# Half-size products for one more up-projection and one more down-projection, attention in pairs of PSUM banks, merged stores and a new order

## The chip, the core and the metric

The kernel runs on one core of one Trainium2 chip. The time is device microseconds of one execution of the whole program. The engines are called PE (TensorE, matmuls; PEld are its weight loads), DVE (VectorE), ACT (ScalarE), POOL (GpSimd, which here only issues the loads and builds one iota) and SP (SyncE, which issues stores and DMA transposes). PSUM has eight banks of 512 fp32 numbers in each of 128 partitions; a matmul writes into one bank.

## What is computed

```python
# q, k, v: [8 batches, 8 heads, 576 positions, 64] fp32; w_in: [512, 2048]; w_out: [2048, 512]
scores = q @ k.T / 8  - slope[h] * |i - j|       # only where 0 <= i - j < 128
attn   = softmax(scores) @ v                     # window of 128
x = attn, heads side by side                     # [4608 tokens, 512]
out = relu(x @ w_in) ** 2 @ w_out                # [4608, 512] fp32
```

## The kernel before

**Tiling.** The tokens are cut into blocks of 128 positions of one batch (the fifth block of a batch has 64; two of these share one tile). Nine groups of four tiles (512 tokens) go through the two projections. Attention of a block multiplies its queries with the keys of its own and of the preceding block: `scores` (L631) fills four PSUM banks `a`, two heads of 256 columns in each; four exponentials (`expo`, L668) and four mask multiplications (`mask`, L675) make `P`; two `pv` steps (L740), each in one bank, multiply with the values and, by a column of ones, give the sums of each row; a reciprocal (L766) and a normalisation (L771) for each of the two write `x`. The first eight blocks, one of each batch, have no predecessor: four of them are done alone (`lone`, L691, with their bias added by a matmul), four in pairs. Their operands are transposed on PE (`tp`, `xp`), those of all later blocks by DMA transposes on SP (L568, L784). A block `m` is numbered in the order in which it is done.

**Up-projection.** `UNITS` and `unit` (L882) do groups 0 to 2 in pieces of 128 or 256 tokens, `fc_step` (L907) groups 3 to 5 in 16 steps of four matmuls of 512 columns. Groups 6 to 8 (`G_UP = 6`) go through `up_product` (L968): a 2 x 2 block product done with seven products of half-size blocks in place of eight (the Strassen-Winograd scheme). Each of four passes `u` has seven products `p`, in the order 1, 2, 6, 5, 7, 3, 4, of four matmuls of 256 columns. The running sums in two PSUM banks X and Y are copied out (`snap`: s1, s2, s5, to `cs` buffers that lie in `vf`, the values of the first blocks) and added to (c11, c22, c12). The block sums of the weights are made once (`up_weight_sums`, L927), those of the tokens for each group (`prepare_up`, L948). `relu_square` (L851) then makes `g` = relu squared: a relu on ACT, a square on DVE or, from group 4 on, on either.

**Down-projection.** Group 0 (`G_STR = 1`) goes through `o_part` (L1054): four tiles x four parts of four matmuls of 512 columns, each part needing only its own quarter of `g` and of `w_out`. Groups 1 to 8 go through `product` (L1126), again seven products, each in two halves of eight matmuls of 256 columns. Products 5, 6, 7 and 4 take sums of quarters of `g`, eight additions on DVE made by `prepare` (L1267): S1, S2, S3, S4; the sums of `w_out` (`wsum`) are made once by `weight_sums` (L1103). Four results are copied to `osb` buffers, three additions finish them, and each tile's half row is stored by one DMA on SP, two where a tile holds two blocks of 64. The last group's product 4 is cut in three (`last_product`, L1230) so that only 128 columns are left at the end.

**What sets the order.** Every step is a task with an engine (or a choice of two), a duration, dependencies, buffers that it takes and gives back (`Slot`) and a key. `Plan.order` (L166) walks through a modelled time and gives each engine, of the tasks that could start next, the one with the smallest key; the resulting order is what each engine's program is. `DUE` gives the first blocks' attention keys near -1e5, loads are near -9e6 and -1e6, projection steps count up from 0. `ADJ` (L54) adds a number written by hand to the keys of some 350 tasks, so `"xp7.0": 129923.5` puts the output transpose of block 7 behind everything that could run. `FIRST` (L17) orders the first loads, all issued by POOL. The `xT` buffer holds three groups: `x` of a tile is written when the up-projection three groups earlier has ended.

PSUM is given out as two banks `h`, one `ox`, one `oy` and four `a` (L342).

Of the kernel before, what the change touches and what calls it, by code (L numbers as in the profile page):

```python
# [38 lines left out]
G_STR = 1  # L39
G_A = 8  # L40
XR = 12
OSB = 5
LAST = 128
G_UP = 6
# [4 lines left out]
RT = 4  # L49
# [5 lines left out]
    "S1.3.0": -903.7, "S1.7.0": 70758.5, "S2.1.0": -1115, "S2.2.1": -558.9, "S2.5.0": 156718, "S3.1.1":  # L55
    105994.9, "S4.1.1": -173131.7, "S4.2.0": 630.1, "S4.5.1": 159840.4, "S4.7.0": 66819.9, "S4.7.1": 198631.5,
    "c22.6.0": -5759.8, "c22.6.2": -2129.9, "c22.7.2": -1777, "c22_4": -255.5, "c22_7": 15343.5, "c22_8":
    -78636.1, "e0.1": 111206.1, "e1.0": 23715.8, "e1.1": -8901146.1, "e11.3": -64325.5, "e12.1": 1217.7,
    "e13.3": 1606.1, "e17.3": 101005.7, "e21.3": 24.9, "e22.1": -48173, "e22.2": -25260.8, "e24.3": 169638.3,
    "e25.1": 163276.8, "e27.1": -198977.9, "e27.2": -1687.7, "e28.0": -234769.8, "e29.1": -301187, "e33.1":  # L60
    124529.3, "e33.2": 227823.7, "e35.3": 124434.7, "e36.1": 10272.4, "e36.2": 2557.9, "e36.3": 7965.3, "e38.2":
    -149, "e38.3": -1670.7, "e6.1": -1247.6, "e9.2": 65398.4, "e9.3": 1738.8, "ev0.1.2": 111234.6, "f6.0.1":
    -988.6, "f6.0.2": -98587.6, "f6.0.3": 116086, "f6.0.5": -98595.7, "f6.0.6": -999.6, "f6.0.7": -13071.6,
    "f6.1.1": -65.1, "f6.1.2": -37683.3, "f6.1.3": -33.7, "f6.1.7": -24308.9, "f6.2.3": 1139.9, "f6.3.2":
    1356.9, "f6.3.3": -316324.9, "f6.3.4": -321979.8, "f7.0.5": 54.9, "f7.1.2": -14751.5, "f7.1.3": 25461.6,
    "f7.1.6": 202.7, "f7.2.3": 25643.8, "f7.2.5": -430.7, "f7.3.2": 244.8, "f7.3.3": 562.7, "f8.0.1": 25806.8,
    "f8.0.3": 520.3, "f8.0.4": 4161.1, "f8.1.3": 30.7, "f8.2.6": -111.1, "f8.2.7": 303.1, "f8.3.3": -159.7,
    "f8.3.4": -94.8, "fc3.1": -41390.5, "fc3.11": -108694.5, "fc3.12": 8034.2, "fc3.13": -177, "fc3.14": 2926.1,
    "fc3.3": -1137.3, "fc3.4": 2862, "fc3.6": -36.5, "fc3.7": -13287.6, "fc3.8": -1157.7, "fc3.9": 11910.5,
    "fc4.0": 12316.7, "fc4.1": 74.1, "fc4.10": 1558, "fc4.11": -1365.7, "fc4.12": 237.6, "fc4.15": -53227.4,  # L70
    "fc4.2": 579.5, "fc4.3": -4010, "fc4.4": -4017, "fc4.6": 267.5, "fc4.7": -1190.4, "fc4.8": -1343.7, "fc4.9":
    -1123, "fc5.1": -184989.8, "fc5.12": -185595.5, "fc5.13": 34045.7, "fc5.14": 896.9, "fc5.15": 734.1,
    "fc5.6": -186223.5, "fc5.7": 661.3, "fc5.9": -186903.9, "kqT16": -174448, "kqT17": 1852.3, "kqT33": -3670.1,
    "kqT34": -2892.3, "lk0.1": 93144.3, "lkq10": -7921038.5, "lkq11": -7921244.2, "lkq12": -7921029.2, "lkq13":
    -7921040.5, "lkq15": -7921000.4, "lkq22": -4.8, "lkq33": 4.3, "lkq36": 181.3, "lkq37": 41384.2, "lkq38":
    -1.7, "lkq8": -7923174.6, "lkq9": -7923136.2, "lv0": -396.5, "lv1": 171.2, "lv10": -7921242.9, "lv20": 3.5,
    "lv28": 993.2, "lv31": 5317.9, "lv36": 41385.5, "lv37": 44238.4, "lv38": 116727.7, "lv39": 41330.6, "lv4":
    1104, "lv6": 75443.5, "lv7": 75344, "lv9": -8025976.9, "m10.0": -1285.4, "m10.1": -30579.1, "m17.0": 2349.5,
    "m17.3": 78002.3, "m21.3": -747.7, "m24.1": 6701.1, "m27.1": 4083.6, "m34.2": 3159.8, "m34.3": 1215.9,
    "m35.0": 1081, "m36.1": 40372.7, "m38.0": 184007.6, "m38.2": 258320.9, "mask0.4": 98879.3, "mask0.5":  # L80
    98879.3, "mask1.3": -1706.3, "mask1.5": -1028.7, "n30.1": 774.5, "n34.0": 10378, "n35.0": 157747.2,
    "o0.0.1": 208.3, "o0.1.2": -72.7, "o0.2.1": 555.9, "o0.3.2": 1297.6, "oe0.0.0": -100128.9, "p1.1.1":
    281063.6, "p1.4.0": 127651.2, "p1.4.1": 879.6, "p2.1.0": -1203, "p2.1.1": 1469.8, "p2.3.0": -41470.3,
    "p2.4.1": 11452.2, "p2.7.1": -1427.4, "p3.1.1": 11949.8, "p3.5.0": 275.6, "p3.6.0": -295, "p3.6.1": -1332.8,
    "p3.7.0": -872.6, "p4.2.0": -1102, "p4.2.1": 92382.6, "p4.3.0": 34421.9, "p4.5.0": 98082.2, "p4.5.1": 476.9,
    "p4.6.0": -213, "p4.6.1": -152.3, "p4.7.1": -508, "p5.2.1": -361.7, "p5.4.0": 62539.3, "p5.5.0": -24602.7,
    "p5.5.1": 463.1, "p6.3.0": 22388.1, "p6.3.1": -722.6, "p6.6.0": 78.7, "p6.6.1": 23875.2, "p6.7.1": 25992,
    "p7.2.0": 4145.8, "p7.3.0": 10821.9, "p7.4.0": 41877.9, "p7.5.1": 43365.4, "p7.6.0": 4154, "p7.6.1":
    43379.9, "p7.7.1": 310.4, "p8.1.0": -76542.9, "p8.5.1": -18573.3, "pv0.1": -23357.1, "pv12.1": -522.7,
    "pv14.0": 625.5, "pv16.1": 1283, "pv19.0": -32.7, "pv19.1": -44115, "pv20.0": 5439.4, "pv20.1": 5438.4,  # L90
    "pv21.0": 9095.4, "pv24.0": -201.1, "pv24.1": -4445, "pv25.1": 1375.7, "pv27.0": 99651, "pv29.1": 92442.5,
    "pv33.0": 481.4, "pv33.1": 3237.8, "pv37.1": 177519.5, "pv4.0": 99332, "pv6.1": 98100.8, "pv7.0": 98916.4,
    "pv7.1": 99166.1, "pv8.0": 164078.1, "r15.0": 1175.1, "r17.1": -6146.6, "r25.1": 3291.9, "r29.0": 4221.8,
    "r30.1": 301.5, "r33.0": -12604, "r35.0": 107764.7, "reluc11.8.2": -274, "reluc12.7.2": -50123.6,
    "reluc12.8.0": 32.4, "reluc22.7.1": -11320.1, "reluf6.3.4": -3847.6, "reluf7.0.4": -10523.3, "reluf7.2.4":
    69.1, "reluf8.1.4": -79957.9, "relufc3.2": -980.7, "relufc3.3": -6110.2, "relufc3.6": -195912.8,
    "relufc4.1": -184059.9, "relufc4.13": -235858.7, "relufc4.2": -5773.1, "relufc5.12": -88019.4, "reluu0.0.3":
    -100507, "reluu0.1.0": -120967.3, "reluu0.1.2": -3207.6, "reluu0.2.0": -99526.1, "reluu2.0.0": 4286.3,
    "reluu2.1.4": -8799.1, "s1.6.1": -1465.9, "s1.7.1": -11303, "s1.7.3": -2349.5, "s18": -769.6, "s1_3":
    -269.1, "s2.6.1": -1027.6, "s2.8.0": -1755, "s20": -7708.7, "s37": 117244.8, "s38": 1255.1, "s5.6.2": -1466,  # L100
    "s5.7.1": -11322.8, "s5.8.0": -209.7, "s5_4": -17186.6, "s5_5": -1045.8, "s8": 1235.4, "sqc11.6.0": 12346,
    "sqc11.6.2": 117202.1, "sqc11.8.2": -61412.6, "sqc11.8.3": 57564.4, "sqc12.6.3": 181517.6, "sqc22.6.0":
    83950, "sqc22.8.1": -88695.8, "sqc22.8.2": 5878.9, "sqf6.1.4": 485.3, "sqf7.0.4": -11305.2, "sqfc4.0":
    55950.5, "sqfc5.12": -1038.8, "squ2.1.6": -663.5, "tp4.0": 99371.5, "tp6.0": 99111.2, "u0.0.4": -888.6,
    "u0.1.3": -790.9, "u0.2.3": -42892.5, "u0.3.3": -937.1, "u1.0.1": -43010.8, "u1.0.3": 31757.8, "u1.0.4":
    -11117.2, "u1.0.6": -10920.4, "u1.1.3": -986.2, "u1.1.4": -910.9, "u1.1.6": -858.6, "u1.1.7": -111184.8,
    "u2.0.0": 219.9, "u2.0.1": 8321.7, "u2.0.2": -57842.5, "u2.0.5": -58325.1, "u2.0.7": -1666.5, "u2.1.0":
    -1151.3, "u2.1.2": -1538.6, "u2.1.3": 110.2, "u2.1.4": -1181.8, "u2.1.5": -1561.6, "u2.1.6": -571.8,
    "u2.1.7": -577.8, "us1.1": 17891.1, "us1.2": 157040.1, "us3.0": -23.7, "us3.1": -21539.9, "us3.3": 2091,
    "ut6.0": -937.1, "ut6.2": -742.1, "w_in0": 532.9, "w_in1": -166.6, "w_in2": -313.3, "w_in3": -413.7,  # L110
    "w_out2": -272.8, "w_out3": 119.4, "x16": 3186.3, "xp5.0": 56027.3, "xp6.0": 99154.6, "xp7.0": 129923.5,
# [18 lines left out]

class Slot:


    def __init__(self, tag):
        self.tag, self.tile, self.left, self.freed, self.idx, self.turn = tag, None, 0, 0.0, 0, 0


class Plan:


    LAT = {"PE": 210.0, "ACT": 180.0, "DVE": 190.0, "POOL": 200.0, "SP": 200.0, "ACTQ": 200.0}
    SELF = {"ACT": 120.0, "DVE": 110.0}
# [123 lines left out]
def kernel(  # L266
# [23 lines left out]
    for b in range(0, B, 2):  # L290
        for x in [(b + i, kb) for i in range(2) for kb in range(1, HALF)]:
            jobs.append(("full", [len(seq)]))
            seq.append(x)
            ranges.append([x])
        jobs.append(("half", [len(seq), len(seq) + 1]))
        seq += [(b, HALF), (b + 1, HALF)]

        ranges.insert(len(ranges) - (b + 2 == B), seq[-2:])
# [58 lines left out]
    def tile_of(slot):  # L357
        return tiles[slot.tag][slot.idx]

    def act(n):  # L360
        return n * 0.832 + 51.0
# [980 lines left out]
```

## Time and profile before

| | us |
|---|---|
| median of three runs (300.56, 301.49, 301.82) | 301.49 |
| the profiled execution's own time | 302.54 |
| its span in the profile | 300.8 |
| PE busy, of the span | 288.8 |
| DVE busy | 243.3 |
| ACT busy | 205.2 |
| POOL busy (issuing loads) | 106.5 |

The profile is that of the one execution in the second row. Busy times are sums over the whole span; the page also cuts the span into 40 slices of 7.5 us and gives each engine's busy share of a slice in tenths. PEclk is the granted clock of TensorE in the same slices. Groups of instructions are listed by line, engine and tiles as count, busy time, mean length of one in ns, idle time before them and who ended it. In the timeline a line has start, length, engine, line, operation, tiles and count, and in brackets the idle time before it. The PE stages by time: group 0 goes up from 15.9 to 34.5 us, group 1 from 49.6 to 71.2, groups 3, 4 and 5 from 118.4, 139.8 and 170.0, groups 6, 7 and 8 from 205.8, 234.5 and 259.6; the last product ends at 295.3.

### The profile page before, as it was taken

How to read it: one execution, taken by the hardware profiler on the slowest of the kernel's cores; microseconds unless marked ns; L12 is line 12 of the kernel's file. 1: busy time of each engine (PE TensorE's matmuls, PEld its weight loads, DVE VectorE, ACT ScalarE, POOL GpSimd, SP SyncE). 2: the span in 40 equal slices, each digit the busy share in tenths (PEclk: the TensorE clock that was granted, in tenths of full speed). 3: DMA queues.
4: the chain of work that ended last, by engine and by line, in shares of the span. 5: the costliest groups of instructions: out<-in, count | busy, mean ns of one | idle time of the engine just before them, and what ended most of it. 6: DMA issues, size and time to landing. Idle time of an engine off the chain costs nothing.

```text
span 300.8 us, 8326 instructions
## 1 busy us (share of the span) xinstructions
PE 288.8 (96%) x3279; PEld 226.2 (75%) x3299; DVE 243.3 (81%) x628; ACT 205.2 (68%) x390; POOL 106.5 (35%) x132
## 2 busy tenths in 40 slices
PE   8799999997999999999999999999999999999992
PEld 4588757886888888556576776568888888888882
DVE  5567568679877899688799997699989998999852
ACT  2685445576487673785978747896979669888710
POOL 8944488445551585522639205510000000000000
PEclk9999999999799999999999999999999999999999
DMA  9999999999999999999999999996103101110213
GB/s 126 170 201 206 181 190 159 164 173 174 174 167 186 123 130 187 164 157 140 167 187 179 160 191 166 152 158 107 37 17 109 38 35 37 70 37 0 80 61 108
DMA packets 170920, 39.62 MB, mean 132 GB/s; under 512 B 156928, under 2 KB 170368, under 8 KB 170880
## 3 DMA queue, kind: packets, MB, share of 16 engines
q0 software_dynamic: 115184, 18.10, 86.5%
q1 hardware_dynamic: 55264, 20.66, 39.2%
q8 instruction: 26, 0.43, 0.6%
q10 hardware_dynamic: 432, 0.33, 0.4%
q14 instruction: 14, 0.11, 0.1%
HBM read 36.70 MB, written 9.44 MB: 153 GB/s over the span
## 4 chain that ended last, share of the span: by engine, by line
PE 85%; DMA 5%; POOL 5%; DVE 2%; issue 1%; POOLq 0%
PE o L1158 33%; PE h L914 14%; PE h L995 12%; PE h L896 10%; PE pv L749 6%; PE s L642 5%; DMA w_in_sb<-in_moe_w_in_dram 5%; PE o L1071 4%; POOL kq L522 2%; POOL vf L527 1%; POOL w_in_sb L467 1%; DVE sums L1281 1%; PE tp L583 1%; PE o L1241 1%; DVE g L869 1%
## 5 line engine op out<-in xcount | busy, mean ns | idle before, releaser
L857 ACT ACTIVATE rt<-h 128x512 bf16<-128x512 f32 (+1 forms) x109 | 64.4, 595 | 30.6 <-PE h L896 14.8
L669 ACT ACTIVATE P<-s 128x512 bf16<-128x512 f32 x120 | 63.6, 604 | 12.7 <-PE s L642 12.7
L1158 PEld LDWEIGHTS <-g 128*128 128x128 bf16 x624 | 59.5, 98 | 8.2
L869 DVE TENSOR_TENSOR g<-rt 128x512 bf16<-128x512 bf16 (+1 forms) x101 | 41.7, 415 | 20.1 <-ACT rt L857 18.6
L522 POOL DMA_DIRECT2D kq<-in_k_dram x39 | 33.2, 852 | 54.0 <-DMA kqT<-kq 47.4
L1158 PE MATMUL o<-w_out_sb,g 128*128 128x256 bf16 x384 | 47.2, 273 | 0.0
L896 PE MATMUL h<-xT,w_in_sb 128*128 128x128 bf16 (+1 forms) x512 | 46.6, 246 | 0.4 <-DMA w_in_sb<-in_moe_w_in_dram 0.4
L914 PE MATMUL h<-xT,w_in_sb 128*128 128x512 bf16 x178 | 45.0, 379 | 0.7
L896 PEld LDWEIGHTS <-w_in_sb 128*128 128x128 bf16 x512 | 38.6, 98 | 4.2 <-DMA w_in_sb<-in_moe_w_in_dram 0.6
L677 DVE TENSOR_TENSOR P<-P,masks 128x512 bf16<-128x512 bf16 x96 | 38.3, 416 | 3.1 <-ACT P L669 1.2
L527 POOL DMA_DIRECT2D vt<-in_v_dram x32 | 27.1, 855 | 31.5 <-PE pv L749 30.7
L522 POOL DMA_DIRECT2D kq<-in_q_dram x39 | 33.6, 862 | 7.7 <-PE h L896 3.2
L1158 PE MATMUL o<-wsum,sums 128*128 128x256 bf16 x256 | 32.9, 279 | 2.1 <-DVE sums L1281 2.1
L777 DVE TENSOR_TENSOR x<-pv,rec 128x256 bf16<-128x256 f32 (+1 forms) x80 | 31.7, 413 | 0.7
L1158 PE MATMUL o<-wsum,g 128*128 128x256 bf16 x240 | 30.7, 273 | 0.0
L1158 PEld LDWEIGHTS <-sums 128*128 128x128 bf16 x256 | 25.1, 100 | 6.6 <-DVE sums L1281 2.3
L914 PEld LDWEIGHTS <-w_in_sb 128*128 128x128 bf16 x192 | 17.2, 98 | 16.6
L749 PEld LDWEIGHTS <-P 128*128 128x128 bf16 (+1 forms) x576 | 23.7, 101 | 6.2 <-issue 0.9
L867 ACT ACTIVATE g<-rt 128x512 bf16<-128x512 bf16 x44 | 27.6, 629 | 1.1
L857 ACT ACTIVATE rt<-vf 128x512 bf16<-128x512 f32 x36 | 22.5, 626 | 6.2 <-DVE vf L1016 5.8
L1016 DVE TENSOR_TENSOR vf<-h,vf 128x512 f32<-128x512 f32 x36 | 24.2, 685 | 2.6 <-PE h L995 2.2
L376 ACT ACTIVATE osb<-o 128x512 f32<-128x512 f32 x21 | 12.6, 598 | 17.1 <-PE o L1158 14.8
(81 smaller groups left out, 393.5 us busy)
## 6 DMA issues: line engine op xcount, KB each, us to landing
out_dram<-osb SPq DMA_DIRECT2D x55, 128.0 KB, 2.7
kq<-in_k_dram POOLq DMA_DIRECT2D x31, 128.0 KB, 7.0
kq<-in_q_dram POOLq DMA_DIRECT2D x31, 128.0 KB, 7.5
vt<-in_v_dram POOLq DMA_DIRECT2D x24, 128.0 KB, 7.5
w_out_sb<-in_moe_w_out_dram POOLq DMA_DIRECT2D x4, 512.0 KB, 14.6
w_in_sb<-in_moe_w_in_dram POOLq DMA_DIRECT2D x3, 512.0 KB, 10.6
out_dram<-osb SPq DMA_DIRECT2D x17, 64.0 KB, 2.1
vf<-in_v_dram POOLq DMA_DIRECT2D x8, 128.0 KB, 6.9
```

Source lines behind the costliest of these rows:

```text
L522: nc.gpsimd.dma_start(view(kq[s_kq[m].idx], i), source(src, m, split))
L527: nc.gpsimd.dma_start(tile_of(s_v[m])[0:n, :, 0:D], source(v, m))
L669: nc.scalar.activation(flat(Pt[sP.idx]), sS[i].tile.rearrange("p (j t) -> p j t", j=2)[:, :, lo:hi], AF.Exp, bias=0.0, scale=scale)
L677: nc.vector.tensor_tensor(flat(Pt[sP.idx]), flat(Pt[sP.idx]), flat(masks), op=ALU.mult)
L749: nc.tensor.matmul(sv.tile[0:n, hi * (D + 1):(hi + 1) * (D + 1)], prob, tile_of(s_v[mk])[:, h, 0:D + 1], start=mk == parts[0][1], stop=mk ...
L777: nc.vector.tensor_tensor(o, heads(sv)[0:n, :, 0:D], sr.tile[0:n, :].unsqueeze(2).to_broadcast([n, 4, D]), op=ALU.mult)
L857: nc.scalar.activation(srt.tile[:, 0:n], i, AF.Relu, bias=0.0, scale=1.0)
L869: nc.vector.tensor_tensor(o, i, i, op=ALU.mult)
L896: nc.tensor.matmul(slot.tile[:, f * w:(f + 1) * w], w_in_sb[:, cc, fc * 128:(fc + 1) * 128], xT[:, cc, lo % (XR * 128):lo % (XR * 128) + w ...
L914: nc.tensor.matmul(slot.tile, w_in_sb[:, cc, fc * 128:(fc + 1) * 128], xT[:, cc, g * 512 % (XR * 128):g * 512 % (XR * 128) + 512], start=c ...
L995: nc.tensor.matmul(slot.tile[:, j * 256:j * 256 + 256], a, b_, start=fresh and j == 0 and c == 0, stop=c == 1, skip_group_check=True)
L1158: nc.tensor.matmul(slot.tile[:, z * 256:z * 256 + 256], stationary(c), moving(c), start=fresh and z == 0 and c == 0, stop=c == F - 1, skip ...
```

## The change

- Group 5 goes up in half-size products too (`G_UP = 5`), and group 0 comes down in them (`G_STR = 0`). The copies' buffers `cs` are four in `vf` and two of their own; one output buffer and one relu buffer fewer (`OSB`, `RT`).
- The four `a` banks become two pairs. One exponential and one mask multiplication cover four heads (1024 columns) in place of two; the two `pv` steps of a block share a pair and have one reciprocal and one normalisation. In the last groups X and Y of a product share a pair. Some products and scores get a dependency that keeps PE's order.
- Stores of two neighbouring tiles are one DMA, and so are the two halves of a tile of 64-row blocks. In the last group the stores of product 3 and of the first 128 columns of the last tile go to ACT's queue, the very last to SP's. The tile with two 64-row blocks of the last batches moves from place 34 to place 32 of 36, so the last two tiles are neighbours.
- All entries of `ADJ` are replaced by others; among the early tasks, those of pv4, pv6, pv7, xp5, xp6 and xp7 are gone, and the iota, the first loads and the squares of group 0 have new ones.

The core of the diff, with entries of `ADJ` that matter early:

```diff
-G_STR = 1
+G_STR = 0
-OSB = 5
+OSB = 4
-G_UP = 6
+G_UP = 5
-RT = 4
+RT = 3
+CS_V = 4
+CS = 6
...
-    "pv4.0": 99332, "pv6.1": 98100.8, "pv7.0": 98916.4, "pv7.1": 99166.1,
-    "tp4.0": 99371.5, "tp6.0": 99111.2, "xp5.0": 56027.3, "xp6.0": 99154.6, "xp7.0": 129923.5,
+    "iota": -12415.8, "lkq1": -13499.7, "lv0": -13699.2, "lv1": -13798.7, "w_in1": -14029.7,
+    "lkq6": 149813.3, "lv4": 149948.7, "lv5": 149915.9, "lv6": 7870399.3, "lv7": 149679.6, "xp4.0": -47745.1,
...
-    psum_bufs = {"h": 2, "ox": 1, "oy": 1, "a": 4}
+    psum_bufs = {"h": 2, "ox": 1, "oy": 1, "a": 2}
...
-        slot.tile = psum.tile([128, 512], FP32, tag=slot.tag, bufs=psum_bufs[slot.tag], name=name)
+        slot.tile = psum.tile([128, 2, 512] if slot.tag == "a" else [128, 512], FP32, tag=slot.tag,
+                              bufs=psum_bufs[slot.tag], name=name)
...
-        sS = [Slot("a") for _ in range(4)]
+        sS = [Slot("a") for _ in range(2)]
...
-            deps = [last["s"]]
+            deps = [last["s"], t_last.get(j - 2)]
...
-        cols = 2 * (hi - lo)
-        for i in range(4):
-            w = slice(2 * i, 2 * i + 2)
+        cols = 4 * (hi - lo)
+        for i in range(2):
+            w = slice(4 * i, 4 * i + 4)
...
+            def norm():
+                nc.vector.tensor_tensor(
+                    xt[sx.idx][0:n, :].rearrange("p (b h e) -> p b h e", b=2, h=4), both()[:, :, :, 0:D],
+                    sr.tile[0:n].unsqueeze(3).to_broadcast([n, 2, 4, D]), op=ALU.mult)
...
+            st["Y"], st["done"] = st["X"] if tag == "a" else Slot(tag), {"before": last.get("s5")}
...
+    def places(r, n):
+
+        rows = [[b * S + kb * 128 for b, kb in ranges[r + i]] for i in range(n)]
+        if n == 2 and len(rows[0]) == len(rows[1]) == 1:
+            lo, d = rows[0][0], rows[1][0] - rows[0][0]
+            if d >= 128 and lo + 2 * d <= NT:
+                return [((0, 1), lambda w: out[lo:lo + 2 * d, w].rearrange("(j p) c -> p j c", p=d)[0:128])]
...
+        if p == 1 and g - 1 in strassen:
+            need = need + [strassen[g - 1]["P", 5, 0]]
+        if p == 5:
+            need = need + [st["P", 2, 0]]
...
+            for i, (j, to) in enumerate(places(4 * g + tok, 2)):
+                def run(j=j, to=to):
+                    (nc.scalar if end else nc.sync).dma_start(
...
+            q = z == 1 and lo == 0
+
+            def store(lo=lo, hi=hi, q=q):
+                to = places(4 * g + 2 + z, 1)[0][1]
+                (nc.scalar if q else nc.sync).dma_start(to(slice(lo, hi)), so.tile[:, z * 256 + lo:z * 256 + hi])
```

## The prediction

> **What bounds the kernel now.** I read the page's busy times and slices first, then the chain of waits, then the stretches and the timeline where the slices dip.
>
> ```profile
> PE 288.8 (96%) x3279; PEld 226.2 (75%) x3299; DVE 243.3 (81%) x628; ACT 205.2 (68%) x390; POOL 106.5 (35%) x132
> ...
> PE   8799999997999999999999999999999999999992
> ...
> DVE  5567568679877899688799997699989998999852
> ...
> PEclk9999999999799999999999999999999999999999
> ```
>
> PE is full in all slices but the first two, the eleventh (about 75 us) and the last. A full slice can still be slow, so I took the pitch of matmuls from long unbroken pieces of the chain (start, length, line, count):
>
> ```profile
> 39.75 1.73 PE o L1071 x8
> ...
> 283.03 10.48 PE o L1158 x96
> ```
>
> A matmul of 512 columns costs 1.73/8 = 0.216 us, one of 256 costs 10.48/96 = 0.109 us. At these pitches the full slices hold little but work: **PE's own work is the bound from 16 to 295 us**. A cut of PE work shows in the end time only if the other engines feed PE as fast as before. Three places are not PE work: the start (to 16 us, untouched in kind), one stall, and the tail after the last matmul.
>
> ```profile
> 71.71 0.69 DVE L1281 TENSOR_TENSOR sums<-g 128x1024 bf16<-128x1024 bf16 x1
> 72.31 0.42 DVE L869 TENSOR_TENSOR g<-rt 128x512 bf16<-128x512 bf16 x1
> 72.65 0.68 DVE L1281 TENSOR_TENSOR sums<-sums,g 128x1024 bf16<-128x1024 bf16 x1
> 73.25 0.69 DVE L1281 TENSOR_TENSOR sums<-g 128x1024 bf16<-128x1024 bf16 x1
> ...
> 73.99 2.52 PE L1158 MATMUL o<-wsum,sums 128*128 128x256 bf16 x16 [2.08 <-DVE sums L1281]
> ```
>
> The first group that is multiplied in half-size products (group 1) makes PE wait 2.08 us for the sums of its operands; behind it the 16 matmuls take 2.52 us where 16 x 0.109 = 1.75 are due, because the granted clock halves (0.79 over 72 to 80 us). Together the stall costs about 3.9 us.
>
> **Products (PE).** Group 0's down-projection: 64 matmuls of 512 columns (64 x 0.216 = 13.86 us) become 7 products of 16 matmuls of 256 columns (112 x 0.109 = 12.23): **-1.63**. Group 5's up-projection is the same exchange: **-1.63**. The weight loads grow by 48 a group at 0.098 us each, but lie beside the matmuls: in the all-product stretch (206 to 283 us) they are busy 68.3 of 77 us and PE is full.
>
> Here a rule speaks against the change. The Trainium skill ("TensorE: Matmul & The Clock Gate", section "Back-to-back issue gap") gives a sustained spacing with weight loads of about 81 ns at 128 columns and 131 ns at 512. An estimate between them, 98 ns at 256, would make each exchange 64 x 0.131 = 8.4 against 112 x 0.098 = 11.0 us, +2.6 a group. The trace contradicts it: 216 and 109 ns, weight loads included.
>
> **Attention in pairs (ACT, DVE).** Rows used (count, busy, mean ns):
>
> ```profile
> L669 ACT ACTIVATE P<-s 128x512 bf16<-128x512 f32 x120 | 63.6, 604 | 12.7 <-PE s L642 12.7
> L677 DVE TENSOR_TENSOR P<-P,masks 128x512 bf16<-128x512 bf16 x96 | 38.3, 416 | 3.1 <-ACT P L669 1.2
> L1281 DVE TENSOR_TENSOR sums<-g 128x1024 bf16<-128x1024 bf16 x16 | 11.0, 687 | 0.4 <-ACT g L867 0.2
> L1016 DVE TENSOR_TENSOR vf<-h,vf 128x512 f32<-128x512 f32 x36 | 24.2, 685 | 2.6 <-PE h L995 2.2
> ```
>
> Four exponentials of 512 become two of 1024. No row has one; the 256- and 512-column relus take 0.384 and 0.599, so 1024 is estimated at 1.03 (between 0.60 and 1.21, two of today's). Over 30 jobs: 30 x (4 x 0.604 - 2 x 1.03) = 10.7 us less ACT. Masks: 120 x 0.416 to 60 x 0.687, -8.7. Reciprocals 72 to 36 at 0.17, -6.1. Normalisations 72 x 0.413 to 36 x 0.685 (the PSUM row), -5.1. DVE -19.9 in all. PE's attention work stays.
>
> **What the products add.** Group 5: 12 additions at 0.685 = 8.2, four token sums at 0.41 = 1.6 (DVE), 12 copies at about 0.64 = 7.7 on either engine. Group 0: eight sums at 0.685 = 5.5, three additions = 2.05; four copies replace four. So DVE stands at about +1, ACT at -7: over the kernel a wash. The place matters.
>
> ```profile
> 170.00:206.00 36.00, 35.74 (x425) 24.73 (x429) 31.39 (x92) 26.12 (x48) 9.31 (x12) 1.00 1.52 166
> 206.00:283.00 77.00, 77.00 (x796) 68.32 (x794) 72.44 (x144) 63.55 (x113) 0.00 (x0) 1.00 0.16 47
> ```
>
> (Columns: length, then busy PE, PEld, DVE, ACT.) Group 5's up-projection runs in the first stretch. DVE and ACT there hold 31.4 + 26.1 = 57.5 us. Add 8.2 + 1.6 + 7.7, take off 1.1 (weight sums that must now come earlier) and 6.7 (nine blocks of attention: 3.8 DVE, 2.9 ACT): 67.2 of 2 x 34.4 = 68.8, or 98%. From 206 to 283 us PE was full with these engines at 136/154 = 88%. Between 88% and 98% lies the risk: nothing, if work slides on; 5.8 us, if all the copies' half share and today's squares stay on DVE (31.4 + 8.2 + 1.6 + 4.1 - 1.1 - 3.8 = 40.2 against 34.4). Nearest is the full-PE row, and squares may go to ACT (L870): I take **+1.0**.
>
> **Early stage.** Group 0's old down-projection was free filler: its 16 parts need no sums. Its new products 5, 6, 7 and 4 need sums on DVE, products 2, 3 and 7 the last of w_out, which landed at 37.5 us. The last up-matmul of group 0 ends at 34.5, its square at 35.6; the two S1 sums with one between (as at 71.71 to 73.94) add 2.2: product 5 starts at 37.9. PE has only product 1 (1.75) and a transpose (0.45) till then, so 1.2 us idle, or 2.9 if product 1 ran earlier, as its counterpart did: I take +2.9. Against it: today block 7's output transpose runs at 61.47, though its operand was ready at 58.5; 24 product matmuls went first, by an order entry of +129923.5 on xp7.0. The entry is gone, as are those on pv4, pv6, pv7 and xp6. Group 1's second half (62.6 to 71.2) can then start about 3 us earlier, and its sums too, while group 0's later products fill: -3.9 for the stall. Sum **-1.0**; from -3.9 (no new stall) to +6.2 (below). Moving the iota behind five load issues (0.87 each) makes the first scores later by some 0.5 and the first loads earlier by 0.5: nothing.
>
> The clock weighs here. The trace halved it for some 3.4 us (0.79 over 8 us) behind a wait of 2.08. The same page of the Trainium skill ("Why this matters for your kernels") warns of gaps over about 3 us only; by that rule neither stall would cost clock, by the row each costs 1.7 more. The -3.9 holds the row's price.
>
> **Tail.** One queue issues the last stores in series:
>
> ```profile
> 293.15 3.21 SPq L1196 DMA_DIRECT2D out_dram<-osb  x5
> 296.47 1.74 SPq L1258 DMA_DIRECT2D out_dram<-osb  x3
> ...
> 295.31 0.29 DVE L1251 TENSOR_TENSOR osb<-osb,o 128x128 f32<-128x128 f32 x1 [0.16 <-PE o L1241]
> ```
>
> DVE is done at 295.60, yet the last issue begins at 297.68 and lands at 299.41. After the change SP has one merged store, then one, then the last; ACT's queue, idle by then, takes three. So the last issue can start at 295.68, as ACT's own did, and land 1.9 us later (median of L1258): 297.6, **-1.8** (-0.8 if ACT's three issues come last, -2.0 at best). Fewer stores elsewhere shorten no path. Four output buffers instead of five and three relu buffers instead of four: a copy then waits for a store of 1.9 to 2.8 us, beside 12 us of PE a group; nothing.
>
> Waits put into PE's order (product 1 behind the previous group's product 5, product 2 behind 1, scores behind the values of two jobs before) follow PE's own order today; queued behind them are later matmuls, and I price them at nothing.
>
> **Sum:** -1.63 - 1.63 + 1.0 - 1.0 - 1.8 = -5.1. The profiled execution took 302.54 (span 300.8 and 1.7 around it), 1.05 above the median 301.49; from the median **296.4**.
>
> **Rivals.** (a) *Starved before 75 us*, slower. Inputs, not PE, set the pace there: the new stall costs 2.9 and 1.7 of clock, the old stall stays and grows by the 1.63 no longer there as filler: +6.2 in place of -1.0, **303.6**. It decides if group 1's sums still end near 73.9. For: loads land one behind another up to 51 us. Against: v7 landed at 51.75, block 7 left its transpose only at 62. Chance 0.15. (b) *DVE is the bound in group 5*: +5.8 in place of +1.0, **301.2**. For: 98%; against: the full-PE row at 88%. 0.15. (c) *Weight loads bound the halved products*: 96 more at 0.098 = +9.4 in place of -3.3, **309**. Against: 0.109 pitch over 96 matmuls. 0.03. The Trainium skill's spacing, above, would bring the same loss at +5.2 in all. (d) *Both early stalls and the pinch vanish*: -2.9 and -1.0 more, **292.5**. 0.08.
>
> **Chances.** Forecast 0.59 (294 to 299.5). Within 0.5% (300.0 to 303.0, about what a measurement can tell from no change) lies most of (b), 0.13; slower are (a) and (c), 0.18; faster 0.69. A range of 292.5 to 301.5 takes in (b) and (d) and leaves out 0.18.
>
> **What would show it.** Right: 112 matmuls a group at L1158 and L995 of 0.109; PE busy down by 3; no idle over 3 us near 35 and none near 73; DVE under 97% while group 5 goes up; last store issued within 0.3 us of the last DVE addition. Wrong: a halved clock before 80 us, PE waiting on `vf` or `sums` between 160 and 240, or exponentials of 1024 above 1.2 us.

## The result, and the profile after

The changed kernel takes **313.54 us** (median of four, 309.79 to 316.18) against 301.02 for the kernel before (four, 300.54 to 301.82): ratio **1.037** (1.028 to 1.047), slower by 3.7% where 296.4 us was forecast. Its profiled execution took 313.18, with a span of 311.4 (before 302.54 and 300.8). Ratios here leave out executions more than 1.5% above the fastest of the same kernel; where a kernel scatters, its other executions are given as well.

The page after the change, busy times and slices:

```profile
PE 289.5 (93%) x3410; PEld 235.7 (76%) x3410; DVE 241.8 (78%) x507; ACT 215.8 (69%) x358; POOL 106.5 (34%) x132
...
PE   6889999999999999999799998978999989989990
...
PEclk9799999999999999999999999999999999999998
```

The stretches (length, then busy PE, PEld, DVE, ACT, POOL; granted clock, DMA share, GB/s):

```profile
0.00:16.00 16.00, 12.23 (x101) 6.99 (x103) 7.18 (x31) 7.09 (x17) 14.91 (x23) 0.89 1.64 149
...
72.00:80.00 8.00, 8.00 (x97) 7.00 (x96) 6.81 (x14) 3.74 (x5) 2.65 (x3) 1.00 2.43 162
...
170.00:206.00 36.00, 34.88 (x434) 29.54 (x432) 33.80 (x67) 30.13 (x49) 13.54 (x17) 1.00 2.08 144
206.00:283.00 77.00, 71.32 (x753) 61.86 (x752) 67.00 (x122) 60.83 (x102) 0.00 (x0) 1.00 0.31 62
```

The old stall at 73 us is gone: 8.00 of 8.00 at full clock, where 6.01 at 0.79 stood. A new dip of the clock stands at the start: behind a wait of 1.37 us for the biases it is 0.50 from 9 to 12 us. What was a full PE from 206 to 283 us now has holes of 5.7 us, and VectorE and ScalarE are *less* busy there than before (67.00 and 60.83 against 72.44 and 63.55). So PE does not wait for their throughput. For what, the list of waits says (us in total, times, longest):

```profile
PE s L640 <- DMA kqT<-kq: 4.6, 2, 2.8
...
PE pv L758 <- DMA vt<-in_v_dram: 1.1, 1, 1.1
PE h L1024 <- DVE cs L1047: 1.0, 3, 0.5
PE h L1024 <- DVE vf L1047: 0.7, 2, 0.5
PE o L1211 <- ACT osb L376: 0.7, 1, 0.7
PE h L1024 <- DVE cs L374: 0.5, 1, 0.5
```

Before, no wait for a transfer stood in this list but 0.4 us at the start, and none at the up-products:

```profile
PE o L1158 <- DVE sums L1281: 2.1, 1, 2.1
...
PE h L896 <- DMA w_in_sb<-in_moe_w_in_dram: 0.4, 1, 0.4
```

Now there are two new kinds: scores and values wait for transposes and loads (5.7 us), and products of groups 7 and 8 for copies and additions of running sums (some 3 us, more with the matmuls' lost overlap).

The merged attention costs what was estimated (1.03 us for the exponential, 0.687 for the mask; count, busy us, mean ns):

```profile
L667 ACT ACTIVATE P<-s 128x1024 bf16<-128x1024 f32 x60 | 58.9, 1021 | 7.3 <-PE s L640 7.3
...
L676 DVE TENSOR_TENSOR P<-P,masks 128x1024 bf16<-128x1024 bf16 x48 | 32.4, 686 | 11.2 <-ACT P L667 11.0
```

The tail grew from 5.5 us behind the last matmul to 7.4. The last issue begins 0.93 us after the last addition, and its landing takes longer still. The last additions and last issues in the timeline, and then, of the issues by size (count, KB, us to landing), the 64 KB store on ACT's queue; the one of the kernel before landed in 1.8 us:

```profile
303.78 0.81 DVE L1312 TENSOR_TENSOR osb<-osb,o 128x256 f32<-128x256 f32 x3
...
303.90 1.53 ACTq L1249 DMA_DIRECT2D out_dram<-osb  x2
305.52 0.38 ACTq L1320 DMA_DIRECT2D out_dram<-osb  x1
```

```profile
out_dram<-osb ACTq DMA_DIRECT2D x1, 64.0 KB, 4.6
```

### The profile page after: what moved, and what is told of

Read it like the earlier page. It is cut to its first block, busy times and chain, and to the rows that moved or that the text cites. A ratio compares the mean times of both kernels' runs of the same rounds, so it can differ in the third digit from the quotient of the medians.

```text
span 311.4 us, 8370 instructions
## 1 busy us (share of the span) xinstructions
PE 289.5 (93%) x3410; PEld 235.7 (76%) x3410; DVE 241.8 (78%) x507; ACT 215.8 (69%) x358; POOL 106.5 (34%) x132
## 4 chain that ended last, share of the span: by engine, by line
PE 64%; DMA 13%; DVE 10%; ACT 5%; POOL 2%; issue 2%; SPq 1%; DVEq 0%; POOLq 0%; ACTq 0%
PE o L1211 24%; PE h L921 12%; PE h L1024 9%; PE h L939 8%; DMA kqT<-kq 6%; PE s L640 5%; PE pv L758 4%; DMA kq<-in_q_dram 4%; DMA vt<-in_v_dram 3%; ACT rt L882 2%; DVE sums L1345 1%; DVE g L894 1%; DVE cs L1047 1%; POOL kq L522 1%; DVE g L1345 1%
## 5 line engine op out<-in xcount | busy, mean ns | idle before, releaser
L1211 PEld LDWEIGHTS <-g 128*128 128x128 bf16 x704 | 67.6, 98 | 10.9 <-issue 0.9
L882 ACT ACTIVATE rt<-h 128x512 bf16<-128x512 f32 (+1 forms) x97 | 57.0, 594 | 26.7 <-PE h L921 15.4
L667 ACT ACTIVATE P<-s 128x1024 bf16<-128x1024 f32 x60 | 58.9, 1021 | 7.3 <-PE s L640 7.3
L522 POOL DMA_DIRECT2D kq<-in_k_dram x39 | 33.3, 854 | 75.5 <-DMA kqT<-kq 63.9
L1211 PE MATMUL o<-w_out_sb,g 128*128 128x256 bf16 x432 | 53.7, 273 | 0.7 <-ACT osb L376 0.7
L921 PEld LDWEIGHTS <-w_in_sb 128*128 128x128 bf16 x512 | 38.4, 98 | 4.0 <-issue 0.6
L676 DVE TENSOR_TENSOR P<-P,masks 128x1024 bf16<-128x1024 bf16 x48 | 32.4, 686 | 11.2 <-ACT P L667 11.0
L892 ACT ACTIVATE g<-rt 128x512 bf16<-128x512 bf16 x55 | 34.3, 629 | 1.5
L939 PE MATMUL h<-xT,w_in_sb 128*128 128x512 bf16 x128 | 31.3, 380 | 0.0
L1024 PEld LDWEIGHTS <-w_in_sb 128*128 128x128 bf16 x256 | 24.4, 98 | 6.1 <-issue 2.8
L1024 PE MATMUL h<-xT,w_in_sb 128*128 128x256 bf16 x192 | 26.9, 273 | 1.1 <-DVE vf L1047 0.5
L802 DVE TENSOR_TENSOR x<-pv,rec 128x512 bf16<-128x512 f32 (+1 forms) x36 | 24.4, 683 | 0.5
## 6 DMA issues: line engine op xcount, KB each, us to landing
w_in_sb<-in_moe_w_in_dram POOLq DMA_DIRECT2D x3, 512.0 KB, 11.2
```

The source lines that it names most:

```text
L522: nc.gpsimd.dma_start(view(kq[s_kq[m].idx], i), source(src, m, split))
L667: nc.scalar.activation(flat(Pt[sP.idx]), sS[i].tile.rearrange("p r (j t) -> p (r j) t", j=2)[:, :, lo:hi], AF.Exp, bias=0.0, scale=scale)
L676: nc.vector.tensor_tensor(flat(Pt[sP.idx]), flat(Pt[sP.idx]), flat(masks), op=ALU.mult)
L882: nc.scalar.activation(srt.tile[:, 0:n], i, AF.Relu, bias=0.0, scale=1.0)
L892: nc.scalar.activation(o, i, AF.Square, bias=0.0, scale=1.0)
L921: nc.tensor.matmul(slot.tile[:, f * w:(f + 1) * w], w_in_sb[:, cc, fc * 128:(fc + 1) * 128], xT[:, cc, lo % (XR * 128):lo % (XR * 128) + w ...
```

## The experiments

Five theories were set against each other. **O**: the new fixed order leaves too little room between a transfer's landing, or a copy, and the product that needs it. **D**: the merged stores hold up the loads, the transposes and the last stores; **H** narrows it to the store of a tile with two 64-row ends (its outer dimension is 2), **M** to the 256 KB stores of two tiles. **C**: VectorE and ScalarE are the bound while groups 5 to 8 go up. **P** came up after the first round: a copy of X waits for products that write Y, since both are now one tile. Except where said, the order of the changed kernel is kept.

### Stores

**All stores single.** Edit, in `store` of the products:

```diff
-                def run(j=j, to=to):
-                    (nc.scalar if end else nc.sync).dma_start(to(w), ...)
+                def run(j=j):
+                    for x in j:
+                        for y, (b, kb) in enumerate(ranges[4 * g + tok + x]):
+                            r, n = b * S + kb * 128, blk[kb]
+                            (nc.scalar if end else nc.sync).dma_start(
+                                out[r:r + n, w], so.tile[64 * y:64 * y + n, x * 256:x * 256 + 256])
```

> Every store of a down-product goes out as before the change, one DMA for each tile of 128 tokens (and for each 64-row half of a tile that holds two sequences); queues and the order of everything else stay as in the changed kernel. Theory O (the new fixed order leaves too little room between the landing of a transfer, or a copy out of PSUM, and the product that needs it): the stores are not the cause, 312.5 to 314.5 us, TensorE's waits for kqT and vt stay (about 6 us) and so do those for the copies. Theory D (merged stores, above all the ones with a slowest dimension of 2, hold up the loads, the transposes and the last stores): the end after the last matmul falls from 7.4 to about 5.5 us, the waits for kqT and vt shrink to under 2 us, 306 to 309 us. Theory C (VectorE and ScalarE are the bound while groups 5 to 8 go up): no change.

Measured: 305.71 us (305.01 to 308.08), ratio 1.0165 (1.010 to 1.023). D holds: 6.2 us by the ratios (1.0372 - 1.0165, of 301). The waits for kqT and vt fall from 5.7 to 2.1 us, and the tail from 7.4 to 4.8 us; that is 3.6 and 2.6 us.

**Only the two-row-end stores apart** (the same edit for `len(j) == 1` alone; two-tile stores stay merged).

> Only the stores of tiles that hold the 64-row ends of two sequences go out as two DMAs of 64 rows again; the two-tile stores of 256 KB stay merged. With every store single the kernel took 305.71 us (the changed kernel 313.54). Theory H (the store with a slowest dimension of 2 runs over two DMA engines only: in the trace some 10 packets of 46 ns in 0.2 us, against 60 to 70 for other stores, and loads and transposes queue behind it): 304.5 to 306.5 us. Theory M (the 256 KB stores hold the queues up): 311 to 314 us. In between, both share the 7.8 us.

Measured: 306.13, 307.25, 310.78 and 311.29 us, ratio 1.0183 (1.011 to 1.026) from the first two. H is favoured, but with half of the executions near 311 this alone didn't settle M. Split, the row-end stores (64 KB) land in 2.1 us in the median; in the changed kernel the 128 KB stores on SP, of which they are a part, took 4.4. The changed kernel's trace shows the store itself. Of these two stretches the first holds only packets of a two-tile store, the second only packets of a two-row-end store:

```profile
230.60:231.40 0.80, 0.80 (x10) 0.71 (x8) 0.80 (x2) 0.44 (x1) 0.00 (x0) 1.00 0.93 328
275.40:276.00 0.60, 0.33 (x3) 0.14 (x2) 0.60 (x2) 0.57 (x2) 0.00 (x0) 1.00 0.13 48
```

The share of the 16 DMA engines is 0.93 at 328 GB/s in one, 0.13 at 48 GB/s in the other: 0.13 x 16 = **2.1 engines**. The Trainium skill ("DMA: Bandwidth & Descriptors", section "Why a DMA increments its semaphore by 16 and not by 1") says that the number of engines is the largest up to 16 that divides the slowest dimension of both sides; with a slowest dimension of 2 that gives two, and the trace agrees. In the tail the same shows: the stretch of the last stores, of the changed kernel and then with single stores:

```profile
305.20:309.80 4.60, 0.00 (x0) 0.00 (x0) 0.00 (x0) 0.00 (x0) 0.00 (x0) 0.93 0.41 114
```

```profile
300.70:303.00 2.30, 0.00 (x0) 0.00 (x0) 0.00 (x0) 0.00 (x0) 0.00 (x0) 1.00 0.77 228
```

The same bytes take twice the time on engines that are half as busy. In the last 1.6 us of the first stretch (308.2 to 309.8) the share is 0.13 to 0.14 at 42 to 49 GB/s, as in the two-row-end store above: about two engines work.

**The two-row-end store in the kernel before**, all else as before (twice, the second time under another name):

```diff
+                    if len(rows) == 2:
+                        d = rows[1][0] - rows[0][0]
+                        lo = rows[0][0] + 64 - d
+                        nc.sync.dma_start(out[lo:lo + 2 * d, w].rearrange("(h p) c -> h p c", p=d)[:, d - 64:d],
+                                          so.tile[:, j * 256:j * 256 + 256])
+                        return
```

> The kernel before with one edit: the store of a tile with the ends of two sequences is one DMA with a slowest dimension of 2, as in the changed kernel, in place of two of 64 rows; order and all else as before. Theory H: the merged store delays transfers here too; the kernel before plans its scores 8 to 14 us behind the transposes, so less of it is seen than the 7.8 us: 302 to 306 us. If it takes the new order for the store to cost anything (theory O): 300.5 to 301.5 us.

> The kernel before with the merged store of the 64-row ends once more: the first time its four executions took 301.67, 307.37, 308.91 and 309.75 us, where the kernel before took 299.95 to 304.37. Theory H: the store delays transfers by a time that changes from run to run, and most executions again lie above 304 us, with TensorE's waits for kqT, xT or vt in the profile. If it was the chip: 300.5 to 302.5 us, as the kernel before.

Measured: of 14 executions seven took 300.6 to 303.2 us and seven 307.4 to 309.8; of 38 of the kernel before beside them the slowest took 304.37. By the ratio, which leaves the long ones out, the second run is the same as the kernel before (1.0043, 1.0008 to 1.0078). The long executions suggest that the store can cost 6 to 7 us in the old order too. That isn't shown: both profiles are of short ones (301.67 and 301.36 us) without a wait for kqT, xT or vt, only four of the second ten lie above 304 where H said most, and kernels without such a store have executions of 306 to 308 us as well (below).

### Late transfers

**Half of the later loads** (the slices `0:H // 2` of k, q from block 16 and of v from block 24 on).

> From block 16 on only heads 0 to 3 of k and q are loaded, and from block 24 on only heads 0 to 3 of v: half the bytes of those loads; the transposes and all arithmetic stay, on stale numbers for heads 4 to 7. It takes away the lateness of the loads and leaves the order alone. Theory O: the waits of the scores for kqT and of the values for vt (about 6 us between 150 and 215 us) go almost wholly, the waits for the copies after 230 us stay: 307 to 309 us. Theory C: the time that TensorE gains there is lost again to VectorE and ScalarE in the same groups, 312 us or more, with VectorE over 97% busy between 170 and 206 us. Theory D: transfers compete with the stores, so the waits go as under O, and the landing of the stores also gets shorter by over 1 us in the median.

Measured: 307.17 us (306.39 to 308.19), ratio 1.0201 (1.015 to 1.026). All waits for kqT and vt are gone (PE 36.00 of 36 us while group 5 goes up), those for the copies unchanged. Taking the bytes out of the loads saves about as much (1.0372 - 1.0201, 5.1 us) as taking the merged stores out, at the same waits. So the loads are late where the merged stores run beside them. The reverse, D's further sign, failed: the stores land as late as before (256 KB in 4.0 us, 128 KB in 4.4).

**Three waits filled by hand**, the order alone:

```diff
+        for late, ahead in (("s26", ("fc4.14", "p3.2.0")), ("pv32.0", ("p4.7.0", "f5.1.4")),
+                            ("s35", ("f6.0.6", "p5.2.1", "f6.0.5"))):
...
+            done[at_late:at_late] = moved
```

> Three waits of TensorE for late transfers are filled by hand: two products that are ready are put ahead of the scores of block 26 (1.73 us), two ahead of the values of block 32 (1.3 us) and three ahead of the scores of block 35 (1.75 us), and nothing else moves. Theory O: the late transfers cost their wait because the in-order queue had ready work behind it, so 4 to 5 us come back, 308.5 to 310 us. Theory C (VectorE and ScalarE are the bound behind it): the waits move to the copies of the same products, 312.5 to 314 us. Theory D: the waits go, the end behind the last matmul stays at 7.4 us; between O and C in time.

Measured: 315.44 us (311.18 to 316.64), ratio 1.039 (1.029 to 1.049): nothing gained, against O. In the profiled execution (316.09) the waits did not go to the copies either (C); other transfers were late instead:

```profile
PE pv L758 <- DMA vt<-in_v_dram: 3.3, 1, 3.3
PE s L640 <- DMA kqT<-kq: 1.5, 1, 1.5
...
PE h L921 <- DMA xT<-x: 1.1, 1, 1.1
```

Why the next transfers were late stays open: POOL's issues of kq stood idle for transposes of kq for 63.9 us of the changed kernel's span (47.4 before), but for 59.6 also in a kernel below in which no transfer is late.

### X and Y in one pair

The trace of the changed kernel around 247 us, unit 1 of group 7 (lines of PE's down-products and of weight loads left out):

```profile
246.94 0.60 PE L1024 MATMUL h<-ut,kqf 128*128 128x256 bf16 x4
...
247.38 0.60 PE L1024 MATMUL h<-xT,w_in_sb 128*128 128x256 bf16 x4
...
248.01 0.60 ACT L376 ACTIVATE cs<-h 128x512 f32<-128x512 f32 x1 [1.32 <-PE h L1024]
...
248.64 0.69 DVE L1047 TENSOR_TENSOR vf<-h,vf 128x512 f32<-128x512 f32 x1 [0.81 <-ACT cs L376]
...
249.39 0.60 PE L1024 MATMUL h<-xT,w_in_sb 128*128 128x256 bf16 x4 [0.54 <-DVE vf L1047]
```

The product at 246.94 finishes s2 in X; the one at 247.38 is product 2, which writes Y. ScalarE is idle, yet copies s2 only at 248.01, when *both* are done. The addition and the next product follow late.

**X and Y in two different pairs** (and single stores, as in the first run):

```diff
-            return slot.tile if X is not Y else slot.tile[:, int(p in (2, 5, 3))]
+            return slot.tile if X is not Y else (X.other if p in (2, 5, 3) else X.tile)[:, 0]
...
+            if p == 1 and X is Y:
+                X.other = bank(slot, "y")
```

> Single stores as in the run that took 305.71 us, and the two accumulators X and Y of the odd products of groups 7 and 8, and of the last down-projection, stand in two different pairs of banks in place of the two halves of one pair. Theory P (a copy of X waits for the products that write Y, since both are one tile: the copy s2 of unit 1 of group 7 starts 0.2 us after the last product of Y, 0.7 us after its own): the waits of L1024 for cs and vf between 245 and 275 us (2.6 us in the list, some 4 with the pitch lost) go, 301 to 303 us. Theory C (VectorE and ScalarE are the bound there): 305 to 306 us. If the order alone is too tight by the durations of the copies (theory O): 304 to 306 us.

Measured: ratio 1.0027 (0.998 to 1.007), by the ratios 4.2 us less than with single stores alone. That rests on six of ten executions (301.57 to 304.51); four took 306.2 to 308.3, and by the median of all ten (303.39) it is 2.3 us. P holds, by the trace. In the trace the same place reads:

```profile
242.88 0.60 PE L1026 MATMUL h<-ut,kqf 128*128 128x256 bf16 x4
...
243.32 0.60 PE L1026 MATMUL y<-xT,w_in_sb 128*128 128x256 bf16 x4
243.52 0.60 ACT L376 ACTIVATE cs<-h 128x512 f32<-128x512 f32 x1 [0.88 <-PE h L1026]
```

The copy starts 0.64 us after its product's first matmul, not 1.07: the four matmuls of product 2 (4 x 0.109) are no longer waited for. All waits of the up-products from 240 us on are gone, with the same work on VectorE and ScalarE, so C falls.

**The same with the merged stores kept.**

> The changed kernel with its merged stores, and only X and Y in two different pairs of banks. Theory P with additive terms: 4 us less than the 313.5 us of the changed kernel, 309 to 310 us. If the late transfers of the merged stores would have hidden those waits anyway: 312 to 313.5 us.

Measured: 312.62 us (310.72 to 313.37), ratio 1.038 (1.033 to 1.043): not additive. The copies' waits are gone here too, but the waits for kqT, xT and vt are 7.2 us in its profile. What it cost is shown by the one kernel that differs from this only in the row-end stores, in two DMAs each (the third of those that compute everything, below): ratio 1.0028, so with X and Y apart the row-end stores alone are worth 10.6 us. The two costs do not add: separate pairs bring nothing while this store is there.

### The start, and what is left

**The iota first** (`done` sorted with the iota ahead), alone and where no transfer is late:

> The iota is issued first on GpSimd again, ahead of the five load issues that the changed kernel puts before it; all else keeps the order. If the 2.2 us that the first scores come later (8.17 against 4.58 us for the biases, the first up-projection 0.9 us later) reach the end: 311.3 to 312.5 us. If the loads of the next blocks, each issued some 0.9 us later behind the iota, hold the first groups up instead: 313 to 314.5 us. Theories O, C and D say nothing of it.

> Single stores, X and Y in different pairs (302.2 us in most runs), and from block 16 on only heads 0 to 3 of k and q, from block 24 on only heads 0 to 3 of v are loaded; all arithmetic stays, on stale numbers for heads 4 to 7. It shows the time of the new order when no transfer is late. If what is left of the loss is late transfers (1.85 us of waits in the profile, with the clock lost behind them): 299 to 300.5 us. If the order itself is too tight for the copies: 301.5 to 302.5 us. The forecast of 296.4 us would need the start, 2 us later than in the kernel before, and the 0.5 us at the last product as well.

> As the run with single stores, X and Y in different pairs and half of the later loads (300.58 us; from block 16 on only heads 0 to 3 of k and q and from block 24 on only heads 0 to 3 of v are loaded, the arithmetic runs on stale numbers for heads 4 to 7), and the iota is issued first. With no transfer late, the start is the largest loss left against the forecast (3 us more waits before 40 us than in the kernel before). If the iota behind the loads is its cause: 298 to 299 us. If it is 0.6 us of it, as the first up-projection showed in the run with the iota alone (15.19 against 15.83 us): 299.8 to 300.3 us, and the rest belongs to the order of the first blocks.

Measured: alone 313.91 us, ratio 1.040: nothing. With half of the loads, single stores and X and Y apart, 300.58 us, ratio 0.999 (0.997 to 1.0015), no wait for a transfer; with the iota first on top, 299.57 us, ratio **0.9935** (0.991 to 0.996). The two ratios differ by 1.7 us, the two medians by 1.0: beside the last run more executions of the kernel before have a mean clock of 0.995 or less (12 of 22, against 9 of 25) and are longer, and the ratio takes that in. Part of the 1.0 is clock too. With the iota late, the profile has a clock of 0.63 from 8 to 12 us, behind a wait of 1.37 us for the biases; the four of its ten executions with a mean clock of 0.998 or more have a median of 300.15 us. With the iota first all seven have 0.996 or more. So the iota behind five load issues costs about 1.0 us, some 0.6 of it without the clock, seen only when nothing else is late.

**Kernels that compute everything.** Iota first and three products ahead of the scores of block 25; iota first alone; two-tile stores merged, row-end stores apart; that with the iota first. X and Y are apart in all four, stores single in the first two.

> The kernel with single stores and X and Y in different pairs, and two edits of the order: the iota first on GpSimd, and three ready products (2.6 us) ahead of the scores of block 25, which waited 2.08 us for their transpose with single stores. If each of the three terms comes back by itself: 0.6 us from the iota, 2.1 us from the scores, 3 to 4 us from the banks: 298 to 300.5 us, below the kernel before. Theory C: 303 us or more. If late transfers only turn up at another place, as they did when three waits were filled at once: 300.5 to 303 us.

> Single stores, X and Y in different pairs, all loads whole, the iota first: the best combination of the parts measured so far that computes everything. If the iota's 0.6 us come back and no transfer is later for it: 301 to 302 us in most executions, the same as the kernel before; below 300 us only if the late transfers (1.85 us of waits) go as well, which nothing here promises.

> X and Y in different pairs, the two-tile stores of 256 KB merged, only the stores of the 64-row ends in two DMAs. With all stores single it took 302.2 us in most runs. If merging two whole tiles is harmless: 301.5 to 303.5 us. If the 256 KB stores delay transfers as well: 304 us or more, with waits for kqT, xT or vt above 3 us in the profile.

> The changed kernel with three edits, everything computed: the stores of the 64-row ends in two DMAs, X and Y in different pairs, the iota first. The first two alone took 301.54 us, without a wait for a transfer in the profile; the iota gave 1.7 us (0.6%) where no transfer was late. If it adds: 299.5 to 300.5 us, a ratio of 0.995 to 0.999 to the kernel before. If loads that start 0.5 us later make a transfer late: 301 to 303 us.

Measured, in that order: ratios 1.018 (1.012 to 1.024; 302.66 to 307.49 us), 1.0026 (0.999 to 1.006; 300.92 to 308.39), **1.0028** (0.999 to 1.006; ten executions of 300.99 to 304.07, median 301.54) and 1.004 (1.000 to 1.008; 300.61 to 307.9). The third shows that two-tile stores are harmless (M falls), and what the order does when no transfer is late:

```profile
80.00:170.00 90.00, 90.00 (x1106) 65.41 (x1105) 70.74 (x148) 67.12 (x98) 44.70 (x54) 1.00 1.77 160
170.00:206.00 36.00, 36.00 (x444) 30.45 (x442) 35.33 (x69) 30.56 (x50) 12.40 (x15) 1.00 1.65 177
206.00:283.00 77.00, 76.25 (x801) 67.17 (x796) 72.14 (x131) 66.66 (x112) 0.00 (x0) 1.00 0.21 51
```

The iota first brings nothing on top of it: five of those twelve executions lie above 304.5 us, and in the profiled one (306.06) kqT, xT and w_in are waited for, 6.1 us. Why is open. It is not that the loads start 0.5 us later: behind the iota the first is issued 0.1 us later (1.34 against 1.25 us), those from the sixth on 0.3 us earlier (5.72 against 6.01). With single stores four of ten executions lie above 305 us with the iota first and without. In the first of the four kernels, the scores of block 25 put back brought waits for the exponentials behind them (1.2 us) and for transposes of x (1.8 us); the time got no better.

**The kernel before with S1 of group 1 ahead of S2** on VectorE:

```diff
+        i, j = names.index("S2.1.1"), names.index("S1.1.0")
+        done.insert(i, done.pop(j))
```

> The kernel before with one edit of the order: on VectorE the second half of S1 of group 1, for which TensorE waits 2.08 us at 73.5 us, goes ahead of the second half of S2 (0.69 us). If that stall is an order of VectorE and not its throughput: the wait falls to about 1.4 us, and the half clock behind it (some 1.8 us lost) may go too: 298.5 to 300.3 us against 301 us. If VectorE is simply full there, the wait moves to the products that need S2: 300.5 to 301.5 us.

Measured: 300.30 us, ratio **0.997** (0.995 to 0.999); nine executions took 299.8 to 300.6, a tenth 591.57, left out. The wait falls from 2.08 to 1.6 us and the clock stays full. It is the only kernel here that computes everything and is below both, by 0.3%. That is the clock: of the executions of the kernel before beside it, the 16 with a mean clock of 0.996 or more have a median of 300.31 us, the same as here, and the 9 with 0.995 or less 301.99.

## Why the prediction was wrong

The forecast's rivals were about engines; the loss came from a store's shape and from a buffer's, and two edits on these bring the changed kernel from 1.037 back to 1.003. In steps of ratios, each between neighbouring runs, in us of 301:

| step | ratio | us |
|---|---|---|
| the changed kernel | 1.0372 | +11.2 |
| stores single | 1.0165 | -6.2 |
| X and Y in two pairs | 1.0027 | -4.2 |
| half of the later loads | 0.9991 | -1.1 |
| iota first | 0.9935 | -1.7 |

The steps hold in this order only, as the run with the merged stores kept showed. Each ratio is known to about 0.005, so the steps to 1 to 2 us; the last is 1.0 by the medians. What is left, -2.0 us (-0.7 against the executions of the kernel before that kept their clock, 300.27 us on the same chip), is the forecast's own part, where it said -5.1.

- **Products, -3.26: size held**, and rival (c) falls. The pitch is as before; the chain of waits ends on this piece, 0.111 us a matmul. The sign that I named, PE busy down by 3, failed (288.8 to 289.5): busy times of overlapped matmuls are modelled, and 15 more fillers run at the start (42 against 27).

```profile
294.25 8.02 PE o L1211 x72
```

- **Pinch in group 5, +1.0: it isn't there.** With transfers in time PE is full from 170 to 206 us (36.00 of 36) with VectorE at 35.33, 98%. Rival (b) falls, and so does my sign "DVE under 97%": 98% cost nothing.
- **Early stage, -1.0: mis-sized, and the new stall was not there.** The old stall went as forecast, and 72 to 80 us is full. The +2.9 was wrong: I left PE only product 1 and a transpose until product 5 had its sums; the trace has 32 matmuls of products that need no sums and eight transposes between 36.29 and 40.23 us. So about -3.9, the outer bound, and rival (a) falls as well.
- **Iota, "nothing": wrong by some 1.0 us.** I set its later start (5.69 in place of 0.84 us) against earlier loads; the identity and the biases wait for it (the first biases at 8.17 us, 4.58 before), and the clock can halve behind that wait. "A halved clock before 80 us" was one of my signs of being wrong; it came, but at 9 us.
- **Tail, -1.8: the failed step that stands nearest to the cause.** The last issue began 0.93 us after the last addition, not 0.1, as three issues of ACT's queue came last (my -0.8 case). The 1.9 us of landing were the median of stores with no such store ahead of them; here they stand behind a store on two engines: 4.6 us came. With single stores the tail is 4.8 us, -0.7.
- **"Fewer stores elsewhere shorten no path": the step that failed outright.** I counted the issues that merging saves and not the engines that a store runs on. The merged stores, by all signs the row-end ones, cost 6.2 us, of which 3.6 were lateness of loads and transposes, far from the stores, and 2.6 the tail; with X and Y apart the row-end stores cost 10.6.
- **"In the last groups X and Y share a pair"** stands in the change and has no term in the sum. It should have been a wait added: what is queued behind the copy is the next product of the same bank, 4.2 us in two groups. "PE waiting on `vf` or `sums`" was listed as a sign, but for another reason and another stretch.
- **The yardstick.** Of the 84 executions of the kernel before that ran beside the experiments, 47 have a mean clock of 0.996 or more and a median of 300.4 us, 37 one of 0.995 or less and 302.0. The profiled one (302.54 us, 0.994) is of the second kind: its stall took the half clock, and I charged that to all. Against the first kind the stall is worth some 2.1 us, the wait alone; my terms as measured (-3.3, 0, -2.1, -0.7) then sum to -6.1, and -0.7 is seen. Even with the iota first, PE is busy for only 34.65 of the first 40 us (36.49 before), 1.8 us less, and waits of 0.5 and 0.25 us stand at the last group's first product and at group 6's end. About 3 us stay unplaced.
- **Small slips in the sums.** 64 x 0.216 is 13.8, not 13.86; the old stall's rows give 2.08 + 1.7 = 3.8, not 3.9; and the worst case of the pinch adds up to 40.4, not 40.2, so rival (b) was 6.0. None decides anything.

## What to carry to other kernels

Merging DMAs saves issues, but the merged pattern decides on how many engines it runs: look at its outermost dimension, and at the DMA share while it runs, before counting the issues saved. When two results are put in one tile, a reader of the one may wait for the writer of the other, though the banks differ; give them separate tiles wherever a copy is on the critical path. And where a fixed order leaves PE few microseconds behind each landing, a slower store elsewhere turns into waits at other places; the one try at filling three of them by reordering PE only moved them. Two such costs can hide each other: measure a fix again after the other one is in.

## What the runs showed of the hardware

- A store with an outermost dimension of 2 ran on about two of 16 DMA engines, 48 GB/s against 328.
- The executions of one kernel can fall into two groups: 300.6 to 303.2 and 307.4 to 309.8 us, seven each, with that store in the kernel before. It isn't the only way there: three kernels without it, with X and Y apart, have four of ten, four of ten and four of twelve above 305 us.
- The clock did not follow the length of a wait alone. It halved behind waits of 1.37 us (the changed kernel, 8 us), 2.08 us (the kernel before), 1.86 us (with X and Y apart and merged stores, 189 us) and 3.31 us (with three waits filled), and stayed at 1.00 behind the same 1.37 us with single stores, behind 2.80 and 1.84 us (the changed kernel) and 2.08 us (single stores). In the kernel before, 37 of 84 executions show the lower mean clock. The two stretches, of the changed kernel behind its 2.80 us and then of the run with three waits filled:

```profile
211.00:213.00 2.00, 1.93 (x29) 1.69 (x29) 0.73 (x2) 1.02 (x1) 0.00 (x0) 1.00 1.14 360
```

```profile
190.00:194.00 4.00, 3.55 (x28) 2.41 (x28) 1.29 (x2) 0.92 (x2) 0.00 (x0) 0.57 2.35 130
```

The prediction charged 1.7 us of clock to every stall; behind the waits of 1.4 to 2.8 us seen here it was lost in some executions and not in others.
